# Exponentials on VectorE: four fused operations a pair, and more banks moved there from ScalarE

## The chip, the cores and the metric

The kernel runs on one core of a Trainium2 chip. The metric is the time of one execution on the device, in microseconds. Five engines of the core matter here: TensorE (PE; its weight loads are listed as PEld), VectorE (DVE), ScalarE (ACT), GpSimd (POOL) and SyncE (SP, which issues most DMAs). Each works through its own queue in order, and they wait for each other by semaphores.

## The reference

Four attention layers over a sequence of 2048 positions and 640 features in bfloat16, each with a layer norm before it and a residual sum behind it. Layers 0 and 2 attend only to the last 256 positions, layers 1 and 3 to all positions, without a mask. There are 32 heads of width 20.

```python
def _B_ref(x, wqkv, wo):
    B, S, D = x.shape
    H = 32
    Dh = D // H
    qkv = (lambda x, *d: x.transpose(*d))((x @ wqkv).reshape(B, S, 3, H, Dh), 2, 0, 3, 1, 4)
    q, k, v = qkv[0], qkv[1], qkv[2]
    scores = jnp.einsum("bhqd,bhkd->bhqk", q, k) * (Dh ** -0.5)
    p = _softmax(scores, axis=-1)
    o = jnp.einsum("bhqk,bhkd->bhqd", p, v)
    return (lambda x, *d: x.transpose(*d))(o, 0, 2, 1, 3).reshape(B, S, D) @ wo
...
x = A_x
x = x + _A_ref(_layernorm(x, axis=-1), A_wqkv, A_wo)
x = x + _B_ref(_layernorm(x, axis=-1), B_wqkv, B_wo)
x = x + _A_ref(_layernorm(x, axis=-1), A_wqkv, A_wo)
x = x + _B_ref(_layernorm(x, axis=-1), B_wqkv, B_wo)
return x
```

`_A_ref` is the same with the mask of 256 positions. A full layer needs 32 x 2048 x 2048 exponentials, twice.

## The kernel before, in words

**Units, banks, tiles.** The work of attention is cut into units `Unit(l, c, g)`: layer l (0 to 3), chunk c of 512 queries (0 to 3), group g of four heads (0 to 7). A *bank* is one bank of PSUM: the scores of one head of the group (j = 0 to 3) for 128 keys (block kc of 16) against the 512 queries, 128x512 values. A unit of a full layer has 16 x 4 = 64 banks. The units of all layers stand in one list: layer 0 first, with parts of layer 1's first chunk woven in, then units of layer 1 with those of layer 2 between them (the stage that the prediction calls the middle), then layer 3.

**The loop.** The banks of all units follow each other and are taken in *tiles* of two, three or four banks, one tile a round of the main loop (L1187). A round with tile t issues, in this order: the score matmuls of the tile (L1221) into PSUM banks 0 to 2 for an even t and 3 to 6 for an odd t, so that two tiles are in flight; the exponential on ACT (L1252), one instruction for all banks of the tile, into a tile `pt` (or, for four banks, into `ka`); some work of the background tasks (`pump`, L1261: projections, normalisation, output projections, all with matmuls, evacuated by DVE through PSUM bank 6); in the middle stage matmuls without a use that keep PE's clock up (`keep_clock`, L613); one step of VectorE's own exponentials (`side_step`, L1263); and then the value matmuls of the group of four banks of an earlier tile (L1288), two to three rounds after their scores, which add up in PSUM bank 7 (`op`). At the end of a unit `op` is copied by DVE (L810), and a background tail divides by the sum of the exponentials (L990 to L1020). Nothing reorders this: each engine gets its instructions as the loop issues them.

**VectorE's exponentials.** In the full layers some banks of the last key block (kc = 15) don't go to ACT: `aside`, heads 2 and 3 in a unit of layer 1, all four heads in a unit of layer 3 (c > 0 in both, but for the first of layer 3 and the last of all). In layer 1 such a bank takes the third place of a tile whose other two go to ACT; in layer 3 its scores have a matmul of their own into bank 6 (L851), in an odd round, whose tile then has three banks and not four. `t_side` (L837) makes the exponentials by pairs of banks: two reads of the scores from PSUM that scale and add and convert to integer (L858), then ten operations on 128x1024 values in f32 that split the number into exponent and fraction and put a polynomial of the fraction in place of the power (L863 to L896). They are issued by a credit: each round adds 0.65 us (in layer 3 1.05, `SIDE_RATE`), each operation takes off what it is thought to cost (0.7 or 1.2). The results lie in buffers `side["out"]`, one in layer 1 and three in layer 3.

**Their value matmuls** (L1297) are issued at the end of the unit, behind its last group. `side_done` (L943) sees to it that their exponentials have been issued by then.

Of the kernel before, what the change touches and what calls it, by code (L numbers as in the profile page):

```python
# [9 lines left out]
BF16 = mybir.dt.bfloat16  # L10
# [5 lines left out]
P = 128  # L16
# [7 lines left out]
C = 512  # L24
# [7 lines left out]

E23 = 2.0 ** 23
LOG2E = 1.4426950408889634
EK, ES, EB, EC, ED = (
    0.34108128280528366, -0.013389613744261132, 0.7155463694844106,
    0.9531181402314826, 0.010462897723623632,
)
KA = 18
SIDE_RATE = 1.05  # L40
QA = 4
# [8 lines left out]
def kernel(  # L50
# [571 lines left out]
    class Unit:  # L622
        def __init__(self, l, c, g, part=None):
            self.l, self.c, self.g, self.part = l, c, g, part
            self.windowed = l % 2 == 0
            self.aside = ()
            if self.windowed:
                sets = [(m, b0, subs, j) for m, b0, subs in window_banks(c) for j in range(4)]
            else:

                if c > 0 and (l, c, g) not in ((3, 1, 0), (3, NC - 1, G - 1)):
                    self.aside = (2, 3) if l == 1 else (0, 1, 2, 3)
                k0, k1 = key_blocks(l, part)
                sets = [
                    (None, 0, [(kc, 0, 4, 0)], j) for kc in range(k0, k1) for j in range(4)
                    if kc < NT - 1 or j not in self.aside
                ]
            n = len(sets)
# [179 lines left out]
    def side_start():  # L818

        assert live["xnT"] == 0  # L820
        tl = [xtp.tile([P, KD, C], BF16, name="xnT", tag="xnT") for _ in range(4)]
        live["xnT"] += 4
        f = [v[:, 0:4, :].rearrange("p a b -> p (a b)") for v in tl[0:3]]
        side["tiles"] = [v.bitcast(F32) for v in f] + [tl[3][:, 0:2, :].rearrange("p a b -> p (a b)")]
        side["out"] = deque(ka_all[:, KA - 6 + 2 * n : KA - 4 + 2 * n, :] for n in range(3))
        side["late"] = True

    def side_early():

        b = part_o["t"]  # L830
        side["tiles"] = [b[:, 2 * n : 2 * n + 2, :].rearrange("p a b -> p (a b)") for n in range(3)]
        side["tiles"].append(b[:, 6, :].bitcast(BF16))
        side["out"] = deque([b[:, 7, :].bitcast(BF16).rearrange("p (a b) -> p a b", a=2)])
        side["gen"] = t_side()
        side_step(False)

    def t_side():  # L837

        V = nc.vector
        while aside:  # L840
            u = aside[0]
            for pair in range(len(u.aside) // 2):
                while id(u) not in loaded or (u.l == 3 and not side["late"]):
                    yield None
                for i in range(2):
                    yield "bank"
                    xi, xm, xw, xe = side["tiles"]
                    if u.l == 3:
                        mseq[0] += 1
                        mfree[6] = (state["tick"] + 2, mseq[0])  # L850
                        nc.tensor.matmul(  # L851
                            ps[:, 6, :], lhsT=u.k(NT - 1, u.aside[2 * pair + i]),
                            rhs=u.q(u.aside[2 * pair + i], 0, 4), start=True, stop=True,
                        )
# [3 lines left out]
                    V.tensor_scalar(  # L858
                        out=xi.bitcast(I32)[:, i * C : (i + 1) * C], in0=side["psum"],
                        scalar1=SCALE * LOG2E * E23, scalar2=127.0 * E23, op0=ALU.mult, op1=ALU.add,  # L860
                    )
                    yield 0.7
                V.tensor_scalar(  # L863
                    out=xm.bitcast(I32), in0=xi.bitcast(I32), scalar1=0x7FFFFF, scalar2=0x3F800000,
                    op0=ALU.bitwise_and, op1=ALU.bitwise_or,
                )
                yield 0.7
                V.tensor_scalar(  # L868
                    out=xi.bitcast(I32), in0=xi.bitcast(I32), scalar1=-0x800000, scalar2=None,
                    op0=ALU.bitwise_and,  # L870
                )
                yield 0.7
                V.tensor_scalar(out=xe, in0=xi, scalar1=0.0, scalar2=None, op0=ALU.max)  # L873
                yield 0.7
                V.tensor_scalar(  # L875
                    out=xm, in0=xm, scalar1=EK, scalar2=ES, op0=ALU.mult, op1=ALU.add
                )
                yield 0.7
                V.tensor_tensor(out=xw, in0=xm, in1=xm, op=ALU.mult)  # L879
                yield 1.2  # L880
                V.tensor_scalar(out=xw, in0=xw, scalar1=EB, scalar2=None, op0=ALU.add)
                yield 0.7
                V.tensor_tensor(out=xw, in0=xw, in1=xw, op=ALU.mult)  # L883
                yield 1.2
                V.tensor_scalar(
                    out=xm, in0=xm, scalar1=EC, scalar2=ED, op0=ALU.mult, op1=ALU.add
                )
                yield 0.7
                while not side["out"]:
                    yield None  # L890
                pt = side["out"].popleft()
                po = pt.rearrange("p a b -> p (a b)")
                V.tensor_tensor(out=po, in0=xw, in1=xm, op=ALU.add)
                yield 1.2

                V.tensor_tensor(out=po, in0=po, in1=xe, op=ALU.mult)  # L896
                side_out.setdefault(id(u), []).append(pt)
                yield 0.7
            aside.popleft()

    def side_step(bank):
# [25 lines left out]
    def side_need(u):  # L927

        if u.l == 3:
            n = 0  # L930
            while u in aside and side.get("scored", {}).get(id(u), 0) < 4:
                n += 1
                assert n < 10000
                side["credit"] = max(side["credit"], 0.1)
# [5 lines left out]
                else:  # L940
                    advance(t)

    def side_done(u):  # L943
        n = 0
        while len(side_out.get(id(u), ())) < len(u.aside) // 2:
            n += 1
            assert n < 10000
            side["credit"] = max(side["credit"], 0.1)
            if side_step(mfree[6][0] <= state["tick"]):
                continue  # L950
            t = choose(False)
            if t is None:
                state["tick"] += 1
            else:
                advance(t)
        return side_out.pop(id(u))

    def s_emitted(u):
        if u.aside:
# [154 lines left out]
    with tc.manual_schedule():  # L1114
# [17 lines left out]
        while n < last_layer:  # L1132
# [1 line left out]
            u = banks[n][0]  # L1134
            at = placed.setdefault(id(u), [])
            extra = []
            if u.aside and len(at) < 2 and banks[n + 1][0] is u and len(tiles) >= 3 * len(at) + (at or [0])[0]:

                extra = [(u, u.aside[len(at)], "side", 0, [(NT - 1, 0, 4, 0)], False, False, False)]
                at.append(len(tiles))  # L1140
                size = 2
            for b in banks[n : n + size]:
# [44 lines left out]
        while ended is None or t < ended + 8:  # L1187
# [3 lines left out]
            if t < len(tiles) or banks:  # L1191
# [81 lines left out]

            u = pts[0][3][0] if pts else None
            size = 4
            if u is not None and u.aside and pts[0][3][4][0][0] == NT - 1:
                size -= len(u.aside)
            if len(pts) >= size and pts[size - 1][0] <= t - (3 if u.windowed else 2):
                group = [pts.popleft() for _ in range(size)]
                subs, end = group[0][3][4], group[-1][3][7]  # L1280
# [4 lines left out]
                for n, (kc, q0, qn, col) in enumerate(subs):  # L1285
                    for _, pg, i, b in group:
                        j = b[1]
                        nc.tensor.matmul(  # L1288
                            op[32 * j : 32 * j + VW, q0 * P : (q0 + qn) * P],
                            lhsT=u.v(kc, j), rhs=pg[:, i, col * P : (col + qn) * P],  # L1290
                            start=(first and n == 0), stop=(last and n == len(subs) - 1),
                            skip_group_check=u.windowed,
                        )
# [65 lines left out]
```

The softmax here doesn't subtract the row's maximum and nothing guards it: scores larger than these inputs give would overflow.

## Time and profile before

| | |
|---|---|
| runs | 2377.62, 2378.59, 2382.4 us; median 2378.59 |
| profiled execution, first to last instruction | 2378.9 us |
| ACT | 2183.4 us busy (92%), 1739 instructions |
| PE | 1980.5 us busy (83%), 15407 instructions |
| DVE | 1458.8 us busy (61%), 2724 instructions |
| exponentials on ACT, 3 banks (L1252, 128x1536) | 1309, 1522 ns each |
| the same, 4 banks (128x2048) and 2 banks (128x1024) | 68, 1965 ns; 193, 1067 ns |
| value matmuls of VectorE's banks (L1297) | 88 and 48 |
| granted TensorE clock, mean | 0.82 |
| HBM | 98.70 MB read, 27.79 MB written |

The page lists busy time by engine, the span in 40 slices (a slice is 59.5 us), the chain of work that ended last, and groups of instructions by source line with their mean duration, followed by the idle time of the engine before them and by what ended it. An instruction's duration can overlap with the next one's on the same engine (ACT's 3-bank exponentials take 1522 ns but start 1.33 us apart), so durations are not simply added where starts are known. A line such as "PE ps L1221 <- ACT pt L1252: 71.1, 157, 0.9" says that PE's instructions of L1221 waited for ACT's of L1252, 71.1 us in all, 157 times, 0.9 us at most. In the timeline the columns are start, duration, engine, line, operation and operands, and in brackets idle time before it with its cause.

### The profile page before, as it was taken

The page shows a single profiled execution, that of the slowest core. Times are in us where ns is not written, and L with a number is a line of the kernel's source. Part 1 is how long each engine was busy: PE and PEld are TensorE (multiplying, and loading weights), DVE is VectorE, ACT ScalarE, POOL GpSimd, SP SyncE. Part 2 cuts the span into 40 slices and gives each one's busy share as a digit, 9 for nine tenths or more (in the row PEclk, how much of TensorE's full clock was granted, in tenths as well). Part 3 has the DMA queues.
Part 4 walks back from the last instruction along what each step waited for, and adds up shares of the span by engine and source line. Part 5 has one row for each costly group of instructions (what it writes and reads, how often), then busy time and mean ns, then how long its engine had stood idle before and what let it go on. Part 6 is the DMA issues. An engine that isn't in the chain of part 4 may idle for free. (4 is left out here: it accounts for less than half of the span.)

```text
span 2378.9 us, 39796 instructions
## 1 busy us (share of the span) xinstructions
PE 1980.5 (83%) x15407; PEld 707.1 (30%) x15554; DVE 1458.8 (61%) x2724; ACT 2183.4 (92%) x1739; POOL 142.5 (6%) x295
## 2 busy tenths in 40 slices
PE   7888988878888888778888888887788788888887
PEld 3443333323322332223322333232221121112122
DVE  7576776425646666656666554452567777777774
ACT  7787889898999999999899999999999989999997
POOL 3110110000000001000110001001000000000000
PEclk9898999997988999999997999899755565556557
DMA  6232422322200223102330034112200010001100
GB/s 183 72 101 63 113 67 59 76 70 64 82 19 26 57 67 93 37 14 54 82 98 20 15 82 113 31 33 75 64 29 26 26 37 26 26 27 37 38 14 12
DMA packets 173678, 132.53 MB, mean 56 GB/s; under 512 B 115760, under 2 KB 156080, under 8 KB 173488
## 3 DMA queue, kind: packets, MB, share of 16 engines
q1 hardware_dynamic: 163872, 101.39, 16.9%
q0 software_dynamic: 9616, 28.59, 3.5%
q8 instruction: 122, 2.00, 0.3%
q14 instruction: 68, 0.56, 0.1%
HBM read 98.70 MB, written 27.79 MB: 53 GB/s over the span
## 5 line engine op out<-in xcount | busy, mean ns | idle before, releaser
L1252 ACT ACTIVATE pt<-ps 128x1536 bf16<-128x1536 f32 (+3 forms) x1584 | 2033.7, 1425 | 149.2 <-PE ps L1221 136.9
L1221 PE MATMUL ps<-qt,kt 32*128 32x512 bf16 x4008 | 657.8, 470 | 214.1 <-ACT pt L1252 153.6
L1288 PE MATMUL ps<-pt,vt 128*21 128x512 bf16 x3688 | 473.1, 464 | 22.9 <-DVE oT L810 13.9
L1221 PEld LDWEIGHTS <-kt 32*128 32x128 bf16 x4008 | 188.9, 94 | 622.2 <-issue 601.3
L1318 DVE TENSOR_TENSOR pt<-pt,masks 128x1024 bf16<-128x1024 bf16 (+5 forms) x403 | 238.9, 625 | 133.4 <-ACT pt L1252 132.8
L353 PE MATMUL ps<-xnT,wqk 128*128 128x512 bf16 x760 | 215.6, 395 | 31.1 <-DMA wqk<-in_B_wqkv_dram 8.7
L1288 PEld LDWEIGHTS <-vt 128*21 128x21 bf16 x3960 | 104.0, 90 | 372.3 <-issue 364.1
L304 DVE CAST st<-ps 128x512 bf16<-128x512 f32 x127 | 87.7, 690 | 165.2 <-PE ps L353 164.2
L530 PE MATMUL ps<-wop,on 128*128 128x320 bf16 x976 | 173.1, 322 | 8.0 <-DVE rz L995 2.8
L613 PE MATMUL ps<-masks,ident 128*128 128x512 bf16 x473 | 167.7, 417 | 6.8 <-issue 3.3
L1221 PE MATMUL ps<-qa,ka 32*128 32x384 bf16 (+2 forms) x1408 | 119.1, 280 | 38.0 <-ACT pt L1252 32.7
L1252 ACT ACTIVATE ka<-ps 128x2048 bf16<-128x2048 f32 x68 | 133.6, 1965 | 2.6 <-PE ps L1221 2.2
L858 DVE TENSOR_SCALAR xnT<-ps 128x512 int32<-128x512 f32 x88 | 60.8, 691 | 120.9 <-PE ps L851 119.6
L1020 DVE TENSOR_TENSOR on<-oT,ps 128x512 bf16<-128x512 bf16 x128 | 87.3, 682 | 64.0 <-PE ps L1016 60.8
L539 DVE TENSOR_TENSOR x_sb<-x_sb,ps 128x320 bf16<-128x320 bf16 x120 | 57.8, 482 | 110.0 <-PE ps L530 109.6
L444 PE MATMUL ps<-wv,xnT 128*128 128x320 bf16 x640 | 113.1, 311 | 7.5 <-DVE va L304 1.5
L810 DVE CAST oT<-ps 128x512 bf16<-128x512 f32 x112 | 76.8, 686 | 67.5 <-PE ps L1288 48.1
L530 PEld LDWEIGHTS <-on 128*128 128x128 bf16 x976 | 91.8, 103 | 77.0 <-issue 40.9
L353 PEld LDWEIGHTS <-wqk 128*128 128x128 bf16 x830 | 72.6, 99 | 124.4 <-issue 54.0
L1288 PE MATMUL ps<-pt,va 128*21 128x384 bf16 (+2 forms) x1408 | 78.9, 287 | 10.7 <-DVE oT L810 4.9
L1221 PEld LDWEIGHTS <-ka 32*128 32x128 bf16 x1408 | 44.8, 92 | 106.5 <-issue 97.8
L1288 PE MATMUL ps<-ka,vt 128*21 128x512 bf16 x272 | 70.0, 600 | 2.6 <-DVE oT L810 1.9
(105 smaller groups left out, 1623.7 us busy)
## 6 DMA issues: line engine op xcount, KB each, us to landing
vt<-v_d SPq DMA_DIRECT2D x48, 336.0 KB
kt<-k_d SPq DMA_DIRECT2D x192, 80.0 KB
wqk<-in_B_wqkv_dram SPq DMA_DIRECT2D x80, 160.0 KB
wqk<-in_A_wqkv_dram SPq DMA_DIRECT2D x70, 160.0 KB
k_d<-st POOLq DMA_DIRECT2D x75, 128.0 KB, 2.2
q_d<-st POOLq DMA_DIRECT2D x75, 128.0 KB, 2.1
qt<-q_d SPq DMA_DIRECT2D x384, 20.0 KB
v_d<-vs POOLq DMA_DIRECT2D x16, 336.0 KB, 3.5
```

Source lines behind the costliest of these rows:

```text
L304: nc.vector.tensor_copy(out=out_, in_=in_)
L353: nc.tensor.matmul(pq, lhsT=wt[:, dc, :], rhs=xt[:, dc, :], start=(dc == 0), stop=(dc == KD - 1),)
L444: nc.tensor.matmul(pv, lhsT=xt[:, dc, i * P : (i + 1) * P], rhs=wv_sb[l % 2][:, dc, h * HD : (h + 1) * HD], start=(dc == 0), stop=(dc == K ...
L530: nc.tensor.matmul(yp, lhsT=on[:, g, qb * P : (qb + 1) * P], rhs=wop[:, g, i * HD : (i + 1) * HD], start=(g == g0), stop=(g == G - 1),)
L613: nc.tensor.matmul(ps[:, b, :], lhsT=ident[:], rhs=masks[:, 0, :], start=True, stop=True)
L810: nc.vector.tensor_copy(out=oT[:], in_=op)
L858: V.tensor_scalar(out=xi.bitcast(I32)[:, i * C : (i + 1) * C], in0=side["psum"], scalar1=SCALE * LOG2E * E23, scalar2=127.0 * E23, op0=ALU ...
L1020: nc.vector.tensor_tensor(out=on[:, g, :], in0=oT[:], in1=zb, op=ALU.mult)
L1221: nc.tensor.matmul(sp[:, i, col * P : (col + qn) * P], lhsT=u.k(kc, j), rhs=u.q(j, q0, qn), start=True, stop=True,)
L1252: nc.scalar.activation(out=pt[:, i:k, b0 * P :], in_=sp[:, i:k, b0 * P :], func=ACT.Exp, scale=SCALE,)
L1288: nc.tensor.matmul(op[32 * j : 32 * j + VW, q0 * P : (q0 + qn) * P], lhsT=u.v(kc, j), rhs=pg[:, i, col * P : (col + qn) * P], start=(first ...
L1318: nc.vector.tensor_tensor(out=pt_[:, i:k, b0 * P :], in0=pt_[:, i:k, b0 * P :], in1=mv_, op=ALU.mult,)
```

## The change

Four things are changed together.

1. The polynomial is another one, of `scalar_tensor_tensor` operations that do two operations on two tensors at once: after two reads of scores and two bit operations, four fused operations follow in place of eight. One buffer less is needed.
2. More banks are moved: in layer 1 all four of the last key block; in layer 3 four for an even g and six for an odd one (two of key block 14).
3. In layer 1 the moved banks are placed 0, 2, 10 and 12 tiles from the unit's first, the credit is 0.8 a round, and there are two result buffers.
4. The value matmuls of a finished pair are issued by `side_values` behind the next group of value matmuls of their unit and no longer at its end. `u.left` counts what is still missing for each head, so that the last one closes the sum.

```diff
-                    self.aside = (2, 3) if l == 1 else (0, 1, 2, 3)
+                    self.aside = tuple((NT - 1, j) for j in range(4))
+                    if l == 3 and g % 2:
+                        self.aside += ((NT - 2, 0), (NT - 2, 1))
...
                     V.tensor_scalar(
                         out=xi.bitcast(I32)[:, i * C : (i + 1) * C], in0=side["psum"],
-                        scalar1=SCALE * LOG2E * E23, scalar2=127.0 * E23, op0=ALU.mult, op1=ALU.add,
+                        scalar1=SCALE * LOG2E * E23, scalar2=-128.0 * E23,
+                        op0=ALU.mult, op1=ALU.max,
                     )
...
                 V.tensor_scalar(
-                    out=xi.bitcast(I32), in0=xi.bitcast(I32), scalar1=-0x800000, scalar2=None,
-                    op0=ALU.bitwise_and,
+                    out=xi.bitcast(I32), in0=xi.bitcast(I32), scalar1=0x7F800000,
+                    scalar2=0x40000000, op0=ALU.bitwise_and, op1=ALU.bitwise_xor,
                 )
                 yield 0.7
-                V.tensor_scalar(out=xe, in0=xi, scalar1=0.0, scalar2=None, op0=ALU.max)
-                yield 0.7
-                V.tensor_scalar(
-                    out=xm, in0=xm, scalar1=EK, scalar2=ES, op0=ALU.mult, op1=ALU.add
-                )
-                yield 0.7
-                V.tensor_tensor(out=xw, in0=xm, in1=xm, op=ALU.mult)
+                V.scalar_tensor_tensor(
+                    out=xw, in0=xm, scalar=EA, in1=xm, op0=ALU.add, op1=ALU.mult
+                )
                 yield 1.2
-                V.tensor_scalar(out=xw, in0=xw, scalar1=EB, scalar2=None, op0=ALU.add)
-                yield 0.7
-                V.tensor_tensor(out=xw, in0=xw, in1=xw, op=ALU.mult)
+                V.scalar_tensor_tensor(
+                    out=xm, in0=xw, scalar=EB, in1=xm, op0=ALU.mult, op1=ALU.add
+                )
                 yield 1.2
-                V.tensor_scalar(
-                    out=xm, in0=xm, scalar1=EC, scalar2=ED, op0=ALU.mult, op1=ALU.add
-                )
-                yield 0.7
+                V.scalar_tensor_tensor(
+                    out=xw, in0=xw, scalar=EC, in1=xm, op0=ALU.add, op1=ALU.mult
+                )
+                yield 1.2
...
-                V.tensor_tensor(out=po, in0=xw, in1=xm, op=ALU.add)
+                V.scalar_tensor_tensor(
+                    out=po, in0=xw, scalar=ED, in1=xi, op0=ALU.add, op1=ALU.mult
+                )
+                side_out.setdefault(id(u), deque()).append((u.aside[2 * pair : 2 * pair + 2], pt))
                 yield 1.2
-
-                V.tensor_tensor(out=po, in0=po, in1=xe, op=ALU.mult)
-                side_out.setdefault(id(u), []).append(pt)
-                yield 0.7
...
+    def side_values(u):
+
+        done = side_out.get(id(u), ())
+        while done:
+            which, pt = done.popleft()
+            for n, (kc, j) in enumerate(which):
+                u.left[j] -= 1
+                nc.tensor.matmul(
+                    op[32 * j : 32 * j + VW, :], lhsT=u.v(kc, j), rhs=pt[:, n, :],
+                    start=False, stop=u.left[j] == 0,
+                )
+            valued[id(u)] += len(which)
+            side["out"].append(pt)
...
-            if u.aside and len(at) < 2 and banks[n + 1][0] is u and len(tiles) >= 3 * len(at) + (at or [0])[0]:
...
+            if (
+                u.aside and len(at) < len(u.aside) and banks[n + 1][0] is u
+                and len(tiles) >= (at or [0])[0] + (0, 2, 10, 12)[len(at)]
+            ):
...
-                side["credit"] = min(side["credit"] + (SIDE_RATE if side["late"] else 0.65), 1.2)
+                side["credit"] = min(side["credit"] + (SIDE_RATE if side["late"] else 0.8), 1.2)
...
-                if end and u.aside:
-                    pair = side_done(u)
-                    for n, j in enumerate(u.aside):
-                        nc.tensor.matmul(
-                            op[32 * j : 32 * j + VW, :], lhsT=u.v(NT - 1, j),
-                            rhs=pair[n // 2][:, n % 2, :], start=False, stop=True,
-                        )
-                    side["out"].extend(pair)
+                if u.aside:
+                    (side_done if end else side_values)(u)
                 if end:
```

In the changed kernel L1221, L1252, L1288 and L613 are L1241, L1272, L1309 and L610; the operations of `t_side` are L863, L869, L874, L879, L883, L887 and L895, the extra score matmul of layer 3 is L857, and the value matmuls of `side_values` are L953.

More of the change, by code (lines that the diff above doesn't have):

```diff
@@ L34 @@
 LOG2E = 1.4426950408889634
-EK, ES, EB, EC, ED = (
-    0.34108128280528366, -0.013389613744261132, 0.7155463694844106,
-    0.9531181402314826, 0.010462897723623632,
-)
+EA, EB, EC, ED = -0.10468731, 1.17604568, 0.83196789, 0.24582313
 KA = 18
@@ L635, in __init__ @@
                     (None, 0, [(kc, 0, 4, 0)], j) for kc in range(k0, k1) for j in range(4)
-                    if kc < NT - 1 or j not in self.aside
+                    if (kc, j) not in self.aside
                 ]
+            self.left = [
+                sum(len(subs) for _, _, subs, jj in sets if jj == j)
+                + sum(jj == j for _, jj in self.aside)
+                for j in range(4)
+            ]
             n = len(sets)
@@ L820, in side_start @@
         assert live["xnT"] == 0
-        tl = [xtp.tile([P, KD, C], BF16, name="xnT", tag="xnT") for _ in range(4)]
-        live["xnT"] += 4
+        tl = [xtp.tile([P, KD, C], BF16, name="xnT", tag="xnT") for _ in range(3)]
+        live["xnT"] += 3
         f = [v[:, 0:4, :].rearrange("p a b -> p (a b)") for v in tl[0:3]]
-        side["tiles"] = [v.bitcast(F32) for v in f] + [tl[3][:, 0:2, :].rearrange("p a b -> p (a b)")]
+        side["tiles"] = [v.bitcast(F32) for v in f]
         side["out"] = deque(ka_all[:, KA - 6 + 2 * n : KA - 4 + 2 * n, :] for n in range(3))
@@ L831, in side_early @@
         side["tiles"] = [b[:, 2 * n : 2 * n + 2, :].rearrange("p a b -> p (a b)") for n in range(3)]
-        side["tiles"].append(b[:, 6, :].bitcast(BF16))
-        side["out"] = deque([b[:, 7, :].bitcast(BF16).rearrange("p (a b) -> p a b", a=2)])
+        side["out"] = deque(
+            b[:, n, :].bitcast(BF16).rearrange("p (a b) -> p a b", a=2) for n in (6, 7)
+        )
         side["gen"] = t_side()
@@ L846, in t_side @@
                     yield "bank"
-                    xi, xm, xw, xe = side["tiles"]
+                    xi, xm, xw = side["tiles"]
+                    kc, j = u.aside[2 * pair + i]
                     if u.l == 3:
@@ L851, in t_side @@
                         nc.tensor.matmul(
-                            ps[:, 6, :], lhsT=u.k(NT - 1, u.aside[2 * pair + i]),
-                            rhs=u.q(u.aside[2 * pair + i], 0, 4), start=True, stop=True,
+                            ps[:, 6, :], lhsT=u.k(kc, j), rhs=u.q(j, 0, 4), start=True, stop=True,
                         )
@@ L863, in t_side @@
                 V.tensor_scalar(
-                    out=xm.bitcast(I32), in0=xi.bitcast(I32), scalar1=0x7FFFFF, scalar2=0x3F800000,
+                    out=xm.bitcast(I32), in0=xi.bitcast(I32), scalar1=0x7FFFFF, scalar2=0x3E800000,
                     op0=ALU.bitwise_and, op1=ALU.bitwise_or,
@@ L930, in side_need @@
             n = 0
-            while u in aside and side.get("scored", {}).get(id(u), 0) < 4:
+            while u in aside and side.get("scored", {}).get(id(u), 0) < len(u.aside):
                 n += 1
@@ L941, in side_need @@
                     advance(t)
+    valued = Counter()
+    def side_values(u):
[10 more added lines that the diff above has]
+            side["out"].append(pt)
     def side_done(u):
         n = 0
-        while len(side_out.get(id(u), ())) < len(u.aside) // 2:
+        side_values(u)
+        while valued[id(u)] < len(u.aside):
             n += 1
@@ L948, in side_done @@
             side["credit"] = max(side["credit"], 0.1)
[L949 to L956, printed above, removed]
+            if not side_step(mfree[6][0] <= state["tick"]):
+                t = choose(False)
+                if t is None:
+                    state["tick"] += 1
+                else:
+                    advance(t)
+            side_values(u)
     def s_emitted(u):
@@ L1136 @@
             extra = []
-            if u.aside and len(at) < 2 and banks[n + 1][0] is u and len(tiles) >= 3 * len(at) + (at or [0])[0]:
-                extra = [(u, u.aside[len(at)], "side", 0, [(NT - 1, 0, 4, 0)], False, False, False)]
+            if (
+                u.aside and len(at) < len(u.aside) and banks[n + 1][0] is u
+                and len(tiles) >= (at or [0])[0] + (0, 2, 10, 12)[len(at)]
+            ):
+                kc, j = u.aside[len(at)]
+                extra = [(u, j, "side", 0, [(kc, 0, 4, 0)], False, False, False)]
                 at.append(len(tiles))
@@ L1275 @@
             size = 4
-            if u is not None and u.aside and pts[0][3][4][0][0] == NT - 1:
-                size -= len(u.aside)
+            if u is not None:
+                size -= sum(kc == pts[0][3][4][0][0] for kc, _ in u.aside)
             if len(pts) >= size and pts[size - 1][0] <= t - (3 if u.windowed else 2):
@@ L1287 @@
                         j = b[1]
+                        u.left[j] -= 1
                         nc.tensor.matmul(
@@ L1290 @@
                             lhsT=u.v(kc, j), rhs=pg[:, i, col * P : (col + qn) * P],
-                            start=(first and n == 0), stop=(last and n == len(subs) - 1),
+                            start=(first and n == 0), stop=u.left[j] == 0,
                             skip_group_check=u.windowed,
                         )
-                if end and u.aside:
-                    pair = side_done(u)
-                    for n, j in enumerate(u.aside):
-                        nc.tensor.matmul(
-                            op[32 * j : 32 * j + VW, :], lhsT=u.v(NT - 1, j),
-                            rhs=pair[n // 2][:, n % 2, :], start=False, stop=True,
-                        )
-                    side["out"].extend(pair)
+                if u.aside:
+                    (side_done if end else side_values)(u)
                 if end:
```

## The prediction

> **What bounds the kernel now.** I read the slices of the page first, then the busy times of two stages, then who waits for whom there, then single instructions. In the slices ACT is at 9 from slice 10 to the end, while DVE has room.
>
> ```profile
> DVE  7576776425646666656666554452567777777774
> ACT  7787889898999999999899999999999989999997
> PEclk9898999997988999999997999899755565556557
> ```
>
> "Middle" is the stage in which units of the second layer (c = 1 to 3) are mixed with the third layer's, "last" is the fourth layer from c = 1 on. Busy times over both:
>
> ```profile
> 790.00:1570.00 780.00, 646.38 (x5470) 246.38 (x5530) 461.04 (x879) 734.71 (x550) 48.22 (x96) 0.93 0.23 58
> 1733.00:2300.00 567.00, 463.51 (x2905) 120.63 (x2902) 412.81 (x598) 548.19 (x388) 0.00 (x0) 0.53 0.10 30
> ```
>
> The columns are PE, weight loads, DVE, ACT, POOL, granted clock. ACT works 94% and 97% of the two stages: the exponentials set the pace. PE is near behind (83% and 82%). The waits say the same: PE waits for ACT to give up a score buffer far oftener than ACT waits for scores. Middle, then last:
>
> ```profile
> PE ps L1221 <- ACT pt L1252: 71.1, 157, 0.9
> ACT pt L1252 <- PE ps L1221: 41.8, 75, 1.5
> ```
> ```profile
> PE ps L1221 <- ACT pt L1252: 48.4, 149, 0.9
> PE ps L1221 <- ACT ka L1252: 39.1, 56, 1.2
> ```
>
> But PE's lead over ACT is at most 0.9 and 1.2 us at any place, so a longer stall of PE reaches ACT. That is what this change must be held against.
>
> **What leaves ACT.** In the built order, banks given to VectorE go from 2 to 4 in each of 24 second-layer units (48 more) and from 4 to 6 in 11 of the 22 last-layer units (22 more). In the last stage, start to start, a tile of 3 banks lasts 1.33 us on ACT (median of 391) and one of 4 lasts 1.76 (median of 68): 0.44 a bank, so narrower tiles (68 tiles of 4 become 47) cost ACT nothing. 22 x 0.44 = 9.8 us. In the middle a 3-bank tile lasts 1.46 in the mean and one with only 2 ACT banks 1.13 (some of these wait for PE), so a bank is worth 0.33 (0.44 if PE always keeps up): 48 x 0.33 = 16 us. **Gain: 26 us, 31 at most.**
>
> **What VectorE pays.** The rows by form:
>
> ```profile
> L879 DVE TENSOR_TENSOR xnT<-xnT 128x1024 f32<-128x1024 f32 x44 | 53.7, 1220 | 0.7
> L868 DVE TENSOR_SCALAR xnT<-xnT 128x1024 int32<-128x1024 int32 x44 | 30.5, 694 | 1.5
> L881 DVE TENSOR_SCALAR xnT<-xnT 128x1024 f32<-128x1024 f32 x44 | 30.4, 690 | 1.0
> ```
>
> A pair of banks costs now nine operations of 0.69 and three of 1.22: 9.87 us. Afterwards: two reads of scores and two bit operations (0.69 each, as L858 and L868) and four scalar_tensor_tensor. That operation is in the trace only at 4 elements (L393). It lies between 0.69 (one f32 input of 1024, L881) and 1.22 (two f32 inputs of 1024, L879); it reads two f32 tensors, so I take 1.22. 4 x 0.69 + 4 x 1.22 = 7.64 us a pair. The sum of DVE's work hardly matters: last stage 44 x 9.87 = 434 us before, 55 x 7.64 = 420 after; middle 24 x 9.87 = 237 before, 48 x 7.64 = 367 after, 130 more on an engine that is 59% busy there.
>
> **What PE now waits for.** Before, the value matmuls of a pair (L1297) are put at the end of its unit. By the built order, the last DVE operation stands 8 or 9 tiles ahead of them in the second layer, and in the last a median of 13. The trace shows what that hides: L1297 waited for L896 once, 2.6 us. After, side_values issues them behind the next value group of that unit. In the built order of the changed kernel the distance is **0 tiles for all 48 pairs of the second layer; in the last 0 for 29 of 55, 1 for 10**. And the pair is done 5 tiles after its second bank was scored in the second layer, 4 in the last (11 and 7 before). PE runs its matmuls in order: behind that value matmul stand the next scores, and ACT waits for those. So two chains race from the scores of the second bank.
>
> DVE: 3 x 0.69 + 4 x 1.22 = 6.95, with 0.03 between operations (863 to 868 in the last stage: 2038.36 to 2039.08) 7.15. Others stand between on its queue, summed from the order with their rows' durations: a mean of 2.27 us in the middle (projections' and normalisation's evacuations, the tail), 0.71 in the last. Two handovers of 0.1 (the score matmul L851 ends at 2037.60, L858 starts at 2037.63; PE's side by estimate). Middle 9.6, last 8.05. Here is how such a chain runs now:
>
> ```profile
> 2051.42 0.69 DVE L858 TENSOR_SCALAR xnT<-ps 128x512 int32<-128x512 f32 x1 [1.60 <-PE ps L851]
> 2052.15 0.69 DVE L863 TENSOR_SCALAR xnT<-xnT 128x1024 int32<-128x1024 int32 x1
> ...
> 2056.92 1.23 DVE L883 TENSOR_TENSOR xnT<-xnT 128x1024 f32<-128x1024 f32 x1
> 2058.13 0.69 DVE L810 CAST oT<-ps 128x512 bf16<-128x512 f32 x1
> 2058.74 0.68 DVE L885 TENSOR_SCALAR xnT<-xnT 128x1024 f32<-128x1024 f32 x1
> 2059.46 1.23 DVE L893 TENSOR_TENSOR ka<-xnT 128x1024 bf16<-128x1024 f32 x1
> ```
>
> It is back to back but for a tail's operation (L810): nothing in it can be pulled forward.
>
> ACT: I matched the score loads, value loads and exponentials of the trace with the built order, tile by tile. From the last score weight load of a tile to the last load of the value group 5 tiles on is 8.23 us in the mean in second-layer units, less 0.33 for the bank that goes: 7.9; then 1.25 (median) until ACT starts the next tile: 9.15. Last, 4 tiles: 6.68 + 1.73 = 8.4.
>
> With the wait, ACT's next tile starts after: score matmuls end 0.4 behind their last load (last: the extra matmul L851, 0.9: load ends 2036.69, matmul 2037.60), the DVE chain, then a pass of the value matmuls and the scores (0.33 + 0.5; last, at half clock, 0.54 + 0.71). Middle 0.4 + 9.6 + 0.8 = 10.8, **1.65 us late, 48 times: 79 us**. Last 0.9 + 8.05 + 1.25 = 10.2, **1.8 late, 29 times, and at distance 1 a tile (1.36) less, 0.45 late, 10 times: 57 us**. PE regains its lead before the next pair (10 tiles in the middle), so I count each.
>
> The same sum for now, in the last stage: 0.9 + 9.18 + 0.3 + 1.3 of others against 7 tiles (11.0) says a last operation ends 0.7 behind its tile's value loads; the trace has 0.85 (median). The method is rather too kind. Over all side operations the trailing is 1.2 us in the middle, 1.5 in the last. Priced by that trailing alone, plus 0.53 for a longer last operation, less PE's slack of 0.4 and 0.5, a pair costs 1.3 and 1.5: 48 x 1.3 + 29 x 1.5 = 106 us in place of 136. At the other end, with 0.69 for the fused operations, the chain is 2.1 shorter and only pairs with over 2.7 us of others are late: some 17 us in all.
>
> The rest is small: one and a half more passes of value matmuls a unit fall into PE's time (0.54 each, spare), 12 fewer filling matmuls, ACT's table and all DMAs as before, one buffer less taken.
>
> **The clock.** In the middle the granted clock falls to half after a stretch in which PE was often idle. From the busy times of two neighbouring stretches:
>
> ```profile
> 1146.81:1150.22 3.41, 1.82 (x20) 0.93 (x20) 2.86 (x7) 2.79 (x2) 0.00 (x0) 1.00 0.47 86
> 1150.22:1157.05 6.83, 6.50 (x39) 2.66 (x37) 4.35 (x8) 5.23 (x4) 0.00 (x0) 0.50 0.01 2
> ```
>
> PE busy 53%, then half clock, ACT 77% busy instead of 94%: 1.2 us lost in 6.8, 0.6 in 3.4. Stalls of 1.7 us can make such stretches: 0 to 48 x 0.6 = 29 us. I leave it out of the sum, since it overlaps with the stalls, and keep it for the range. The Trainium skill (TensorE: Matmul & The Clock Gate, Part 1) has the clock throttled only after a window of about 3.4 us idle; by that these stalls cost nothing in clock. The stretch above was not idle and the clock fell, and the last stage sits at 0.53 with PE 82% busy, so the rows speak against the page here.
>
> **Sum.** 79 + 57 - 26 = +110 us on a span of 2378.9 (the median of the runs, 2378.59, is the same within 0.3): **2489 us**.
>
> **Rivals.**
> 1. *The waits are hidden; faster.* The fused operations run at 0.69, or PE arrives later than I think (its background tasks are behind in the middle). For it: ACT's idle time was small although DVE trailed. Against: two f32 inputs cost 1.22 in every row. 2378.9 - 26 + 17 = 2370, down to 2348 with no stall at all.
> 2. *Half the stalls only*: PE, late already in many middle tiles, meets a finished operand: only the last stage pays. 2378.9 + 57 - 26 + some = 2410 to 2440.
> 3. *The clock goes too*: after each middle stall PE stays at half clock, and late value matmuls delay the next pair; 2489 + 29, and where others trail as they do now (there 1.0 behind in the median, where the same sum says 2.3 ahead, since DVE waits for other products of PE), up to 48 x 1 more: 2520 to 2580.
> 4. *No change*: stalls of 0.5 us would eat the gain; nothing ties it there.
>
> The point that decides between faster and slower: a mean stall of 0.34 us a pair of the 77 at distance 0 (26 / 77).
>
> **How the numbers follow.** Slower as priced, 2440 to 2520: 0.58. Rival 2: 0.13. Rival 3: 0.15. Rival 1: 0.11. Rival 4, within 0.2% (about what a measurement can tell): 0.03. Slower 0.86, faster 0.11, same 0.03. The range takes the likeliest case, most of rival 3 and rival 2 from 2415: 2415 to 2570.
>
> **What would show it.** Right: waits of the value matmuls at L953 for DVE L895, about 1.5 to 2.5 us each, 48 on raw_o and some 30 on ka; ACT waiting for L1241 some 130 us more; middle ACT share near 85%; clock there below 0.93. Wrong: L895 near 0.69 us, or L953 idle under 30 us in all, or ACT still 94% and 97% busy.

## The result, and the profile after

The changed kernel takes **2556.59 us** (median of four, 2556.15 to 2556.89) against 2380.04 for the kernel before in the same comparison: a ratio of **1.0722, 95% interval 1.0686 to 1.0759**. The forecast was 2489 with a range of 2415 to 2570.

Below, "middle" is the stretch from ACT's first exponential of the first mixed tile (layer 1, c = 1, with layer 2) to the last one's end, 543.3 to 1557.5 us in the kernel before and 544.8 to 1690.2 in the changed one; "last" is layer 3 from c = 1 on, 1686.8 to 2366.4 and 1821.9 to 2542.0. Outside these two the kernels differ by some 4 us. The middle went from 1014 to 1145 us, the last from 680 to 720.

First the slices of the page (busy tenths of DVE and ACT, granted clock of PE):

```profile
DVE  6667765346666676766676664543477666666663
ACT  6787989887888778888778869999999989998887
PEclk9999999988877797767887689989665565556556
```

In slices 10 to 22 (counted from 0), where ACT stood at 9 (once at 8), it is now at 7 or 8, and the clock, there at 8 or 9 before (once at 7), is at 6 or 7 in nine of these thirteen. (A slice is now 63.9 us, not 59.5.) DVE is a little busier, but nowhere full. Busy times of the two stages in the changed kernel (PE, weight loads, DVE, ACT, POOL, clock):

```profile
544.80:1690.20 1145.40, 935.03 (x6969) 318.67 (x7053) 726.82 (x1241) 944.64 (x738) 56.72 (x112) 0.81 0.19 49
1821.90:2542.00 720.10, 569.05 (x3528) 149.83 (x3528) 472.61 (x617) 647.22 (x460) 0.00 (x0) 0.56 0.09 27
```

ACT did less (945 us in the middle against 954), in much more time: its share fell to 82%. Who made it wait? PE's waits in the middle and in the last stage, then ACT's in the middle:

```profile
PE ps L953 <- DVE raw_o L895: 61.0, 44, 3.3
PE ps L1309 <- DVE oT L814: 17.8, 19, 1.8
```
```profile
PE ps L953 <- DVE ka L895: 50.3, 32, 4.4
```
```profile
ACT pt L1272 <- PE ps L1241: 185.7, 185, 3.8
```

The new line is L953, the value matmuls of VectorE's pairs: they wait 44 times in the middle (1.4 us in the mean) and 32 times in the last stage (1.6). ACT's waits for scores grew from 56 to 186 us. One such stall in the timeline (start, duration, engine, line):

```profile
1160.88 4.16 ACT L1272 ACTIVATE pt<-ps 128x1536 bf16<-128x1536 f32 x3
...
1163.30 0.44 PE L1309 MATMUL ps<-pt,vt 128*21 128x512 bf16 x4
1163.36 0.09 PEld L953 LDWEIGHTS <-vt 128*21 128x21 bf16 x1
1164.29 0.20 DVE L1025 COPY rT<-ps 32x128 bf16<-32x128 bf16 x1
1164.43 1.21 DVE L895 SCALAR_TENSOR_TENSOR raw_o<-raw_o 128x1024 bf16<-128x1024 f32 x1
1165.69 0.58 PE L953 MATMUL ps<-raw_o,vt 128*21 128x512 bf16 x2 [1.95 <-DVE raw_o L895]
...
1166.20 0.61 PE L1241 MATMUL ps<-qt,kt 32*128 32x512 bf16 x3
...
1167.20 1.45 ACT L1272 ACTIVATE pt<-ps 128x1536 bf16<-128x1536 f32 x1 [2.15 <-PE ps L1241]
```

PE has loaded the weights at 1163.36, and when its earlier matmuls are done (1163.74) it stands until L895 ends at 1165.64. The next tile's scores stand behind it in program order, so ACT, which ran dry at 1165.04, starts at 1167.20. And the clock follows. The busy times of the stretch that ends there and of the next one:

```profile
1162.34:1165.75 3.41, 1.46 (x17) 0.46 (x15) 3.08 (x5) 2.70 (x3) 0.00 (x0) 1.00 0.00 0
1165.75:1179.40 13.65, 13.18 (x69) 3.66 (x69) 7.33 (x12) 8.96 (x8) 0.00 (x0) 0.50 0.02 4
```

PE was busy 43% of 3.41 us; then it has half its clock for 13.65 us, and ACT is busy 66% of that time. In the whole middle the clock was at half for 427 us, against 170 before.

### The profile page after: what moved, and what is told of

Same layout as the page of the kernel before. It is cut to its first block, busy times and chain, and to the rows that moved or that the text cites. A ratio compares the mean times of both kernels' runs of the same rounds, so it can differ in the third digit from the quotient of the medians.

```text
span 2554.7 us, 39812 instructions
## 1 busy us (share of the span) xinstructions
PE 2091.2 (82%) x15392; PEld 708.1 (28%) x15542; DVE 1576.8 (62%) x2732; ACT 2170.3 (85%) x1738; POOL 142.4 (6%) x295
## 5 line engine op out<-in xcount | busy, mean ns | idle before, releaser
L1272 ACT ACTIVATE pt<-ps 128x1536 bf16<-128x1536 f32 (+2 forms) x1604 | 2051.3, 1374 | 338.4 <-PE ps L1241 312.2
L1241 PE MATMUL ps<-qt,kt 32*128 32x512 bf16 x3986 | 687.5, 492 | 149.2 <-ACT pt L1272 114.3
L1309 PE MATMUL ps<-pt,vt 128*21 128x512 bf16 x3702 | 486.2, 488 | 37.4 <-DVE oT L814 26.6
L1241 PEld LDWEIGHTS <-kt 32*128 32x128 bf16 x3986 | 172.9, 95 | 589.6 <-issue 573.5
L350 PE MATMUL ps<-xnT,wqk 128*128 128x512 bf16 x761 | 227.1, 412 | 29.7 <-DMA wqk<-in_B_wqkv_dram 9.9
L1309 PEld LDWEIGHTS <-vt 128*21 128x21 bf16 x3890 | 102.2, 91 | 397.1 <-issue 391.1
L527 PE MATMUL ps<-wop,on 128*128 128x320 bf16 x976 | 183.7, 336 | 12.5 <-DVE x_sb L536 4.9
L610 PE MATMUL ps<-masks,ident 128*128 128x512 bf16 x457 | 172.3, 439 | 11.3 <-issue 3.8
L863 DVE TENSOR_SCALAR xnT<-ps 128x512 int32<-128x512 f32 x110 | 76.1, 692 | 168.4 <-PE ps L857 155.6
L1241 PE MATMUL ps<-qa,ka 32*128 32x384 bf16 (+2 forms) x1408 | 119.5, 281 | 40.3 <-ACT pt L1272 35.5
L441 PE MATMUL ps<-wv,xnT 128*128 128x320 bf16 x640 | 118.6, 322 | 8.8 <-DVE rz L1012 2.1
L814 DVE CAST oT<-ps 128x512 bf16<-128x512 f32 x112 | 76.6, 684 | 72.7 <-PE ps L1309 71.0
L863 DVE TENSOR_SCALAR raw_o<-ps 128x512 int32<-128x512 f32 x96 | 66.0, 688 | 65.7 <-PE ps L1241 56.8
L1272 ACT ACTIVATE ka<-ps 128x2048 bf16<-128x2048 f32 x47 | 90.4, 1923 | 0.5 <-PE ps L1241 0.4
L1309 PE MATMUL ps<-pt,va 128*21 128x384 bf16 (+2 forms) x1408 | 80.3, 292 | 10.7 <-DVE oT L814 4.8
L1241 PEld LDWEIGHTS <-ka 32*128 32x128 bf16 x1408 | 44.5, 92 | 108.1 <-issue 100.7
```

What stands on the lines that cost most here:

```text
L350: nc.tensor.matmul(pq, lhsT=wt[:, dc, :], rhs=xt[:, dc, :], start=(dc == 0), stop=(dc == KD - 1),)
L441: nc.tensor.matmul(pv, lhsT=xt[:, dc, i * P : (i + 1) * P], rhs=wv_sb[l % 2][:, dc, h * HD : (h + 1) * HD], start=(dc == 0), stop=(dc == K ...
L527: nc.tensor.matmul(yp, lhsT=on[:, g, qb * P : (qb + 1) * P], rhs=wop[:, g, i * HD : (i + 1) * HD], start=(g == g0), stop=(g == G - 1),)
L610: nc.tensor.matmul(ps[:, b, :], lhsT=ident[:], rhs=masks[:, 0, :], start=True, stop=True)
L814: nc.vector.tensor_copy(out=oT[:], in_=op)
L863: V.tensor_scalar(out=xi.bitcast(I32)[:, i * C : (i + 1) * C], in0=side["psum"], scalar1=SCALE * LOG2E * E23, scalar2=-128.0 * E23, op0=AL ...
```

## The experiments

Times of stages are those of the one profiled execution of each kernel. The four kernels with two banks a unit in the second layer and nothing added there (before, three rounds later with two banks, fused operations alone, candidate) have 1014 to 1022 us in the middle, so that under 10 us mean nothing there. The last stage repeats more closely: five kernels with the same order in it have 680.6 to 681.5 us, three others 720 to 725. Ratios are to the kernel before.

| kernel | ratio (95% interval) | middle, us | last, us | half clock in the middle, us |
|---|---|---|---|---|
| before | 1 | 1014 | 680 | 170 |
| changed | 1.0722 (1.0686 to 1.0759) | 1145 | 720 | 427 |
| values at the unit's end | 1.0283 (1.0254 to 1.0312) | 1060 | 701 | 311 |
| the same in the second layer alone | 1.0374 (1.0341 to 1.0406) | 1056 | 725 | 297 |
| waits filled | 1.0573 (1.0541 to 1.0604) | 1105 | 724 | 235 |
| kernel before, early values | 1.0090 (1.0057 to 1.0123) | 1022 | 691 | 178 |
| values three rounds later | 1.0195 (1.0163 to 1.0227) | 1050 | 681 | 275 |
| values one round later | 1.0222 (1.0198 to 1.0245) | 1059 | 690 | 282 |
| three rounds later, two banks | 1.0028 (1.0010 to 1.0046) | 1016 | 681 | 171 |
| three rounds later, clock target | 1.0212 (1.0173 to 1.0251) | 1064 | 682 | 319 |
| fused operations alone | 0.9989 (0.9973 to 1.0005) | 1022 | 668 | 209 |
| two banks and idle work | 1.0109 (1.0086 to 1.0131) | 1031 | 681 | 188 |
| four banks, half the work | 1.0206 (1.0184 to 1.0227) | 1057 | 681 | 303 |
| candidate | 0.9997 (0.9981 to 1.0012) | 1017 | 674 | 190 |

**Values at the unit's end.**

```diff
-                if u.aside:
-                    (side_done if end else side_values)(u)
+                if u.aside and end:
+                    side_done(u)
```

> The changed kernel with its value matmuls of VectorE's banks put back to the end of their unit; the fused operations and the additional banks stay. By the built order the distance from a pair's last operation to its value matmuls goes from 0 tiles to 5, 6, 15 or 16 in the second layer, and in the last layer 12 of 55 pairs are left at 0 or 1. Theory 1 (PE stalls at these matmuls, and the clock falls with the stalls): nearly all of the 176 us goes, the middle stage comes back to 990 to 1020 us (1012 before, 1144 after) at a clock of 0.9 or more, the last to 665 to 685; total 2345 to 2375 us. Theory 2 (VectorE's load is the trouble: 127 us more of its work in the middle, evacuations of PSUM come late whatever the place of the value matmuls): the middle stays above 1070 us, total above 2440.

Both theories fall as they stood. The waits at L953 are gone in the middle, and 86 of its 131 additional us with them, but 45 stay: more than theory 1 and less than theory 2 allows (the total, 2449, is above the 2440 of theory 2). In the last stage 25.3 us of waits (9 of them) remained, at pairs that are finished just as their unit ends.

**The same in the second layer alone**: `if u.aside and (end or u.l == 3)`.

> The same, but in the second layer alone: in the last the value matmuls stay behind the next group. It shares the loss out between the stages. Theory 1: the middle stage comes back to 990 to 1020 us, the last stays at about 718 us; total 2395 to 2425. Theory 2: middle above 1070, total above 2480.

The stages are independent: the middle is that of the run above, the last that of the changed kernel. The total is over what theory 1 allowed by just the 45 us that stay in the middle.

**Waits filled.**

```diff
         done = side_out.get(id(u), ())
+        if done and u.l == 1 and mfree[6][0] < 1 << 30:
+            for _ in range(5):
+                nc.tensor.matmul(
+                    ps[:, 6, :], lhsT=ident[:], rhs=masks[:, 0, :], start=True, stop=True
+                )
         while done:
```

> The changed kernel with five filling matmuls in front of the value matmuls of 45 of the 48 pairs of the second layer, into PSUM bank 6: PE is busy where it waited (1.4 us in the mean), and nothing else changes. If the fall of the granted clock (0.92 before, 0.81 after in the middle) is a cause of its own beside the 61 us of waits: clock back to 0.87 or more, middle 30 to 90 us shorter, total 2465 to 2525. If the waits alone are it, and the low clock only goes with them: no gain; the same to 30 us slower, 2550 to 2590.

Its middle:

```profile
548.30:1653.40 1105.10, 921.29 (x7177) 332.99 (x7282) 726.12 (x1241) 939.20 (x738) 56.70 (x112) 0.89 0.20 51
```

PE does 225 matmuls more for nothing, the clock is 0.89 and not 0.81, and the stage is 40 us shorter, although the value matmuls can start no earlier after their exponentials. The low clock is a cause of its own, worth some 40 us of the 131; it may be more, since half clock still lasts 235 us and not 170.

**The kernel before with early values**: its `side_done` at the unit's end replaced by `side_values` of the change, all else as it was.

> The kernel before (its eleven operations, 2 and 4 banks a unit), with this one part of the change: the value matmuls of a finished pair stand behind the next group of their unit. Distance 0 tiles for 16 of 24 pairs of the second layer and 24 of 44 of the last, 1 for 8 and 7. Theory 1: slower than before, by less than the whole change, as the chain has 11 and 7 tiles from the second bank: trailing 1.0 and 0.85 us less PE's slack of 0.4 and 0.5, some 24 x 0.6 + 24 x 0.35 = 23 us, up to 60 with the clock; 2395 to 2440. Theory 2: as before, 2375 to 2385, since VectorE's work is the same.

2403.77 us, 21 more than the kernel before; 23 had been worked out from the trailing of its last operation. (A pair has twelve operations there, not eleven.) PE waits for these operands 10.1 us in the middle and 15.2 in the last stage. The distance costs by itself, and less a pair than in the changed kernel; that the chain has more tiles here (11 and 7 after the second bank, not 5 and 4) is the reason that the expectation gives.

**Values three rounds later.** A pair's round is stored with it, and `side_values` passes over younger ones:

```diff
-        while done:
-            which, pt = done.popleft()
+        while done and done[0][2] <= state["round"] - wait:
+            which, pt, _ = done.popleft()
...
-                    (side_done if end else side_values)(u)
+                    side_done(u) if end else side_values(u, 3)
```

> The changed kernel, but a finished pair's value matmuls wait in the program until three rounds after its last operation (distance 3 or 4 for all 48 pairs of the second layer and 0 to 2 for 4 of 55 of the last, by the built order), and do not go to the end of the unit. Theory 1, for the last layer (only the distance matters there): waits at these matmuls under 15 us (50 in the changed kernel, 25 with the end of the unit), last stage 665 to 685 us against 679 before and 700 with the end of the unit. Middle as with the end of the unit, 1050 to 1065; total 2400 to 2435. If the last stage stays at 700 or more, something other than these waits costs there.

The busy times of its middle and last stage:

```profile
544.20:1594.60 1050.40, 896.28 (x7057) 312.44 (x7057) 724.60 (x1241) 939.65 (x738) 57.69 (x112) 0.87 0.21 53
1723.90:2404.60 680.70, 562.73 (x3528) 145.12 (x3528) 471.50 (x617) 645.87 (x460) 0.00 (x0) 0.57 0.09 28
```

The waits at L953 are 5.2 us (two) in the last stage and none that count in the middle. 39.4 us of the last stage and 95 of the middle were the place of the value matmuls, with the clock that it cost. Yet with less work for ACT the last stage is only where it was before the change, and the middle is 36 us longer.

**Values one round later**: the same with `side_values(u, 1)`.

> The kernel three rounds later with one round in place of three: distance 1 for 32 of 48 and 31 of 55 pairs. One tile is 1.36 us in the last layer, where the waits at distance 0 were 1.6 us in the mean (50 us, 32 times). If they shrink by the tile: waits of 10 to 25 us in the last, its stage 683 to 700 us, middle 1055 to 1090; total 2430 to 2470, between distance 3 (2428) and 0 (2557).

10.3 us of waits in the middle, 9.4 in the last, against 61.0 and 50.3. One tile takes away most of the loss, not all: the last stage is 690 us and not 681. The total does not differ from distance 3 beyond the intervals.

**Two banks** in the second layer, their old places and credit, values three rounds later.

> As the kernel three rounds later, with two banks a unit in the second layer as before the change (and their old places and credit); fused operations stay, the last layer keeps four and six. What is left in the middle after the waits are gone (1060 us against 1014 before) is put to the test. If it comes with the two additional banks (VectorE's work there 725 us against 599, or the tiles of two banks): middle 1000 to 1015, total 2350 to 2390. If it comes with the fused operations or the early value matmuls themselves: middle above 1035.

**Two banks and idle work.** Behind each pair of the second layer two bit operations and four fused ones on scratch:

```diff
+                if u.l == 1:
...
+                    for _ in range(4):
+                        V.scalar_tensor_tensor(
+                            out=xw, in0=xm, scalar=EA, in1=xm, op0=ALU.add, op1=ALU.mult
+                        )
+                        yield 1.2
```

> Two banks a unit leave ACT in the second layer (as in the kernel with two banks), but behind each of its 24 pairs VectorE does six more operations of the same kinds on scratch, which nobody reads: 2 x 0.69 + 4 x 1.22 = 6.3 us, nearly the work of a second pair. The credit is 0.8. Only VectorE's load is that of four banks; the tiles and ACT's work are those of two. Theory A (VectorE's queue: evacuations, op's copy and the normalisation come late, PE waits and its clock falls): middle 1040 us or more (1016 with two banks, 1051 with four). Theory B (the tiles with two ACT banks: ACT is done with them in 0.89 us and PE can't follow): middle 1010 to 1025.

**Four banks, half the work.** The second pair's chain is left out but for its reads and the last operation:

```diff
+                full = u.l == 3 or pair == 0
+                if full:
...
-                    out=po, in0=xw, scalar=ED, in1=xi, op0=ALU.add, op1=ALU.mult
+                    out=po, in0=xw, scalar=ED, in1=xi if full else xw, op0=ALU.add, op1=ALU.mult
```

> The reverse: four banks a unit leave ACT in the second layer as in the kernel three rounds later, but VectorE makes the exponentials of the first pair alone; of the second it does the two reads and one fused operation on old values, 24 x 5.0 us less. The second pair's exponentials are left out of the computation. Theory A: middle 995 to 1020 us (two banks less for ACT are then worth something). Theory B: 1040 to 1055, as with all of the work.

The middle of these three, in this order:

```profile
543.50:1559.40 1015.90, 867.27 (x7069) 313.61 (x7069) 552.11 (x1049) 954.35 (x738) 56.43 (x112) 0.92 0.21 55
```
```profile
546.40:1577.80 1031.40, 854.19 (x6984) 314.12 (x7069) 692.50 (x1193) 956.34 (x738) 58.58 (x112) 0.91 0.21 54
```
```profile
544.70:1602.00 1057.30, 890.93 (x6973) 312.20 (x7057) 610.18 (x1121) 940.21 (x738) 56.68 (x112) 0.86 0.21 53
```

The 36 us come with the additional banks, their places and their credit, not with the fused operations: two banks are back at 1016. VectorE's load accounts for a part: 140 us more of it behind two banks costs 15 us (between the bounds of theories A and B, and 1.0109 against 1.0028 in the totals), and PE's waits for VectorE rise there from 57 to 69 us; the credit differs too, 0.8 and not 0.65, and is not told apart from the load here. The larger part belongs to the four-bank order itself: with 114 us of VectorE's work taken out the stage does not come back (1057), although ACT has 14 us less to do than with two banks. What the profile shows of it is a lower clock (half for 303 us, against 171 with two banks) and one wait, of the next unit's first value matmuls for the copy of `op`. Its rows, two banks and then four with half the work:

```profile
PE ps L1310 <- DVE oT L814: 5.0, 14, 0.7
```
```profile
PE ps L1312 <- DVE oT L814: 16.7, 17, 1.8
```

This wait goes with the order and not with VectorE's load: with two banks and idle work it is 4.7 us. With four banks, in 12 of 55 cases in the middle, the copy of `op` (L814) runs directly behind the second bit operation of the next unit's first pair; with two banks it never runs directly behind an operation of a pair. One case with four banks and half the work:

```profile
652.57 0.69 DVE L871 TENSOR_SCALAR raw_o<-raw_o 128x1024 int32<-128x1024 int32 x1
...
653.29 0.69 DVE L876 TENSOR_SCALAR raw_o<-raw_o 128x1024 int32<-128x1024 int32 x1
653.90 0.68 DVE L814 CAST oT<-ps 128x512 bf16<-128x512 f32 x1
...
654.63 0.40 PE L1312 MATMUL ps<-pt,vt 128*21 128x512 bf16 x4 [1.76 <-DVE oT L814]
```

With four banks the pair's second bank stands two tiles behind the first and not three. That this brings the two together is likely, but not shown, and how much of the 36 us comes from it (the wait itself is 12 us longer) no run has tested.

**Clock target.** `keep_clock(1.0 * (n_b + side_tile) - surplus)`: a tile's third bank counts for the filling though it does not go to ACT.

> As the kernel three rounds later, with one line changed: the filling matmuls that keep PE's clock up count the bank that VectorE gets, so that a tile with two ACT banks aims at 3.0 and not at 2.0. If the low clock of the middle (310 us at half clock with the value matmuls at the end, 170 before) comes from too few fillings in the 96 such tiles: half clock under 220 us, middle 1000 to 1035, total 2360 to 2400. If it comes from waits of PE on a loaded VectorE: half clock stays above 270 us and the middle at 1050 to 1075.

The clock is no higher: 319 us at half. But the edit hardly added fillings. Their weight loads, in the kernel three rounds later and then here:

```profile
L610 PEld LDWEIGHTS <-ident 128*128 128x128 bf16 x537 | 35.5, 99 | 86.9 <-issue 85.5
```
```profile
L610 PEld LDWEIGHTS <-ident 128*128 128x128 bf16 x541 | 36.5, 100 | 88.9 <-issue 86.9
```

Four more of 537, so that neither expectation was put to the test. (PE's busy time of 915 us in the middle against 896 goes with the lower clock.) Whether more fillings would help, and why half clock lasts longer in the four-bank order, stays open.

**Fused operations alone**: two and four banks, old places, values at the end.

> The fused operations alone: two and four banks a unit and the old places and credit as before the change, value matmuls at the end of their unit. VectorE does 68 x 2.23 = 152 us less work. If ACT sets the pace and VectorE is off the path: 2370 to 2385, no difference of more than 0.3%. If VectorE's queue costs in the kernel before too (its copies of PSUM come earlier when it has less to do): 2340 to 2370.

The total is the same, as the first expectation had it. Its last stage, however, is the shortest of all:

```profile
1699.70:2367.80 668.10, 551.52 (x3528) 155.99 (x3528) 390.38 (x529) 650.41 (x461) 0.00 (x0) 0.56 0.10 29
```

VectorE works 390 us there and not 482, and PE waits for it 7 us and not 17. The copy of `op` stood directly behind an operation of a pair in 12 of 23 cases there before the change, and here in one. The reason of the second expectation holds for this stage, where ACT's work is the same as before; its 12 us don't show in the total, since the middle is 7 us longer (within what such kernels scatter by) and begins 5 us later.

**Candidate**: fused operations, two banks in the second layer, six in 6 of 22 units of the last (`g % 4 == 1`), values three rounds later.

> What the runs point to: the fused operations, two banks a unit in the second layer, six in a quarter of the last layer's units (6 of 22) and four in the others, values three rounds later. Against the kernel before: middle 1010 to 1020 (the same), last stage 660 to 668 us (668 with the fused operations alone, less 12 x 0.44 = 5); total 2365 to 2378, faster by 0.2 to 0.6%. If VectorE's queue costs again what leaves ACT: 2378 to 2386.

No faster than the kernel before. Set beside its neighbours it gives the price of the banks: with 0, 12 and 22 banks over four a unit the last stage takes 668, 674 and 681 us, and VectorE works 390, 436 and 472. By the prediction ACT loses 0.44 us of work with each bank; the stage gets 0.6 longer with each. From 0 to 12 the place of the value matmuls changes as well (at the unit's end, three rounds later); from 12 to 22 the banks alone do, and it is 0.7.

## Why the prediction was right in its sign and short in its size

The **race of two chains** was right. The order said distance 0 for 48 and 29 pairs; the profile has 44 and 32 waits at L953, taking the value matmuls away from there takes 95 us from the middle and 39.4 from the last stage, and doing that alone to the kernel before costs 21 us where 23 follow from the same reasoning. The fused operation takes 1.22 us, as taken. ACT's waits for scores grew by 130 us in the middle and 44 in the last stage, where the prediction's signs have some 130 in all.

**Where the time lies.** 2557 us is in the range, but above the likeliest case (2440 to 2520). It is in the prediction's rival 3 (2520 to 2580, chance 0.15), whose first half, PE at half clock after the stalls, is what happened; of its second half, later stalls, nothing shows (1.4 us in the mean, less than the 1.65 reckoned). The number is partly luck: two terms below missed by 16 and 18 us in opposite directions, and nearly all of the distance between +110 and +176 is the gain that did not come.

**Last stage, stalls: 57 us said, 39.4 found.** The mean wait was 1.6 us where 1.8 had been reckoned as a loss of ACT, and ACT recovered part of it: without these waits PE stands 45 us less at L953, and ACT waits 38 us less for scores (32 and not 70).

**Middle, stalls: 79 us said, 95 found**, but made up otherwise: 61 us of waits, not 48 x 1.65, and, as far as the filled waits show (40 us), the clock for the rest. The step "I leave it out of the sum, since it overlaps with the stalls" was a wrong one. Half clock grew by 257 us; with PE filled at the same waits the stage is 40 us shorter. The price of 0.6 us a stall was that of 3.4 us at half clock; in the changed kernel 40 stretches at half clock began in the middle where there had been 23, and 21 of them lasted 10 to 31 us where 7 had (10 to 14 us).

**The gain: 26 us said, nothing found.** The step that failed is to price a bank by ACT's time alone ("Gain: 26 us"), and with it "The sum of DVE's work hardly matters". Beside the stalls, the additional banks cost 36 us in the middle, some 15 of them by VectorE's load, the others by an order whose cost is measured but only in part explained, and 13 in the last (681 against 668, with the values in another place), where the fused operations had given 12. VectorE is 59% to 71% busy in these stages and still not off the path: PE's next value matmuls wait for its copies of PSUM (L814), some of which stand behind the operations of a pair.

Put together: 95 + 39.4 for the place of the value matmuls, 36 for two more banks in the middle, 13 - 12 for the last stage; some 172 of 176 us. These are the steps from the changed kernel over others to the one before, so that they must add up to the two stages' difference; the sum shows where the time went, and is no test of the causes.

## What to carry to other kernels

Ask of each instruction that waits across engines how far behind its producer it stands in the order of issue: at distance 0 it stops an engine that works in order and everything queued behind it; at a distance of one tile it cost PE some 10 us of waits in a stage here, and not 50 to 60. Don't price work moved to an engine by that engine's average idle time; price it by who waits for the short operations that now queue behind the long ones, and test it by adding idle work of the same size. Count what an edit added before reading its result: the clock target added four matmuls. Where an engine's clock falls after idle stretches, as PE's did here, a stall can cost more than its length (95 us for 61 us of waits).

## What the runs showed of the hardware

- Half clock came after stretches in which PE was idle for a third to a half of the time: in the 3.41 us before each fall in the middle, 1.24 us of idle time in the mean before the change (23 falls) and 1.55 after (40), never less than 0.7. The Trainium skill (TensorE: Matmul & The Clock Gate, Part 1) has it after an idle window of about 3.4 us, and further down in that part also from frequent short idle times; no wholly idle window lay before these falls, so that the rows go against the first, which is all that the prediction took from the page, and not against the second. How much idle time it takes is not shown: in the kernel three rounds later, falls came after stretches with PE 37% to 82% busy, and 32 full-clock stretches of 3.41 us with PE under 75% busy were not followed by one.
- At half clock PE was 97% busy for 13.65 us (1165.75 to 1179.40) before the clock came back; what brings it back is not shown.
- scalar_tensor_tensor with two f32 inputs of 128x1024 takes 1.22 us, with f32 or bf16 output, as tensor_tensor with two f32 inputs does (L879 before the change, 1.22).
- A weight load is taken ahead of a waiting matmul (1163.36, its matmul 1165.69), a matmul is not: the Trainium skill (TensorE: Matmul & The Clock Gate, Part 2) says so too.
